# One ring of 17 half-size places for the second product's reads, eight steps ahead, and TensorE's order there as written

## The chip, the cores and the metric

One core of a Trainium2 chip runs the whole kernel. The time is the device time of one execution in microseconds (us), taken as the median of several; the kernel before has a median of 612.07 us over three runs (610.14 to 614.16). The engines are named as the profile names them: PE is TensorE's matrix multiply, PEld its weight load, DVE VectorE, ACT ScalarE, POOL GpSimd, SP the queue that issues nearly all DMAs here.

## The reference

Retention attention (a linear attention with a decay per head), and after it a feed-forward layer whose activation is `h * relu6(h + 3) / 6`:

```
state = gamma * state + outer(k_t, v_t);  y_t = scale * q_t @ state      # 4 batches, 8 heads, 768 tokens, 64 wide
x = y laid out as (3072 tokens, 512)
h = x @ w_in                      # (3072, 2048)
g = h * clip(h + 3, 0, 6) / 6
out = g @ w_out                   # (3072, 512)
```

All in float32.

## The kernel before

**Number format.** TensorE multiplies in the chip's reduced fp32r format. `split` (L130) turns a float32 tile into a high part (ACT, L131) and a low part, the rest (DVE, L132), and every product of two tiles is three matmuls: high by high, high by low, low by high. One matmul here is 128x128 weights by 512 columns.

**First product (up to L369).** Tokens are taken in six units of 512. Attention makes x for a unit, in pieces, between the matmuls of the unit before. `mm1` (L328) makes one 128x512 tile of h in 12 matmuls; ACT and DVE turn it into g (L337, L338), and SP stores it to DRAM (L339), into `gd[j]`, where j counts 8 pairs of 128 rows, at the place of the token unit and of the half (0 or 1) of the pair. PE's order is fixed to the order of the code there (`manual_schedule`, L343, closed at L368). The last unit's matmuls end at about 364 us.

**Second product (from L372).** It is done for three pairs of token units (u, v) by a scheme with seven instead of eight block products. A pair goes through four sweeps s, and a sweep through the eight j; one (pair, sweep, j) is a *step*:

- s = 0 reads g(u,0) and g(u,1), and makes products 1 and 2 from them
- s = 1 reads g(v,0), g(v,1), g(u,0); DVE makes s1 = g(v,0) + g(v,1), s2 = s1 - g(u,0), s3 = g(u,0) - g(v,0); products 6 and 7 from s2 and s3. s1 and s2 stay in `keep`
- s = 2 reads g(u,1); DVE subtracts s2; products 5 and 3 from s1 and that difference
- s = 3 reads g(v,1) for two j in one step; product 4

So a pair has 8 + 8 + 8 + 4 = 28 steps, and each step is two 128x512 operands, split into four tiles (one `gc` of 128x2x2x512), and 12 matmuls: 84 steps, 1008 matmuls. When a sweep ends, `evict` (L457) adds its PSUM banks into output tiles on ACT and DVE, and stores those that are complete.

The reads (`load_g`, L384) go into three kinds of tile: `gr` (two operands of 512 columns, 512 KB, two buffers in the pool `late`) for s = 0 and 3, `gr2` (three operands, two buffers) for s = 1, `gr3` (one, two buffers) for s = 2. `gc` has four buffers, two in each of the pools `late` and `rest`. `late` lies in memory that is free before the last token unit (L354); `rest` opens after the first product's pools are closed, and a tile of it waits for what lay at its place (`reuse_waits="tile"`).

The first two steps are read and split ahead of everything (L500, high priority); two more are read (L504), and then the loop at L507 prepares step n + 2 and reads step n + 4 with each step n (`SOON, FAR = 2, 4`, L486). DVE's instructions for them are placed behind `end`, the last DVE instruction of the first product (`issue_after`). The order of each engine's and queue's instructions, PE's in the second product too, is made by a scheduler from priorities, its own estimates of durations and the buffers that are free; every engine and SP then takes its instructions strictly in that order, and an instruction that waits holds up those behind it.

Of the kernel before, what the change touches and what calls it, by code (L numbers as in the profile page):

```python
# [9 lines left out]
F32 = mybir.dt.float32  # L10
# [9 lines left out]
P = 128  # L20
# [8 lines left out]
def retention_ffn(ctx: ExitStack, tc: tile.TileContext, qkv, w_in, w_out, dvs, dqs, out, B, H, S, D):  # L29
# [6 lines left out]
    nc = tc.nc  # L36
# [8 lines left out]
    UT = UR * P  # L45
# [16 lines left out]
    gd = [dram.tile([P, NU, 2, UT], F32, name=f"gd{j}") for j in range(NFP)]  # L62
# [8 lines left out]
        out=mask, in_=mask, pattern=[[1, P]], compare_op=ALU.is_ge, fill=0.0, base=0, channel_multiplier=-1  # L71
# [8 lines left out]
    def nm(s):  # L80
        return f"{s}_{next(serial)}"

    def dve_sub(out_, a, b):
        return nc.vector.tensor_tensor(out=out_, in0=a, in1=b, op=ALU.subtract)  # L84

    def dve_add(out_, a, b):
        nc.vector.tensor_tensor(out=out_, in0=a, in1=b, op=ALU.add)  # L87
# [42 lines left out]
    def split(hi, lo, src):  # L130
        nc.scalar.activation(out=hi, in_=src, func=AF.Copy)  # L131
        nc.vector.tensor_tensor(out=lo, in0=src, in1=hi, op=ALU.subtract)  # L132
# [187 lines left out]
    def advance(n):  # L320

        nonlocal done
        while done < min(n, NROW + 2):
            next(gen)
            done += 1
# [16 lines left out]
    order = ExitStack()  # L342
# [8 lines left out]
    for n, (u, jj) in enumerate(steps):  # L351
        if (u, jj) == (NU - 1, 0):
            att.close()
            late = ctx.enter_context(tc.tile_pool(name="late", bufs=1, side="right", reuse_waits="tile"))  # L354
# [10 lines left out]
            advance(2 * UR + 2 + int((jj + 1) / NF * UR + 0.5))  # L365
        elif 1 < u < NU - 1:
            advance(UR * (u + 1) + 2 + int((jj + 1) / NF * UR + 0.5))
    order.close()  # L368
    ph1.close()  # L369


# [4 lines left out]
    rest = ctx.enter_context(tc.tile_pool(name="rest", bufs=1, reuse_waits="tile"))  # L376
# [4 lines left out]
    work = [(b, s, j) for b in range(NB) for s in range(4) for j in range(0, NFP, 1 + (s == 3))]  # L381
    raws, gcs, banks, outs = {}, {}, {}, {}

    def load_g(step):  # L384

        b, s, j = step
        if s == 1:
            t = rest.tile([P, 3, UT], F32, tag="gr2", name=nm("gr2"), bufs=2)
            nc.sync.dma_start(out=t[:, 0], in_=gd[j][:, 2 * b, 0])
            nc.sync.dma_start(out=t[:, 1:3], in_=gd[j][:, 2 * b + 1])  # L390
        elif s == 2:
            t = rest.tile([P, UT], F32, tag="gr3", name=nm("gr3"), bufs=2)
            nc.sync.dma_start(out=t, in_=gd[j][:, 2 * b, 1])
        else:
            t = late.tile([P, 2, UT], F32, tag="gr", name=nm("gr"), bufs=2)
            if s == 0:
                nc.sync.dma_start(out=t, in_=gd[j][:, 2 * b])
            else:
                for i in range(2):
                    nc.sync.dma_start(out=t[:, i], in_=gd[j + i][:, 2 * b + 1, 1])  # L400
        raws[step] = t

    def sums(step):

        b, s, j = step
        t = raws.pop(step)
        s1, s2 = keep[j], keep[NFP + j]
        if s == 1:
            a11, a21, a22 = (t[:, i] for i in range(3))
            s3 = rest.tile([P, UT], F32, tag="s3", name=nm("s3"), bufs=2)  # L410
            dve_add(s1, a21, a22)
            dve_sub(s2, s1, a11)
            dve_sub(s3, a11, a21)
            raws[step] = (s2, s3)
        elif s == 2:
            dve_sub(t, t, s2)
            raws[step] = (s1, t)
        else:
            raws[step] = t

    def split_g(step, n):

        t = raws.pop(step)
        gc = (late, rest)[n // 2 % 2].tile([P, 2, 2, UT], F32R, tag="gc", name=nm("gc"), bufs=2)
        if isinstance(t, tuple):
            for i in range(2):
                split(gc[:, i, 0], gc[:, i, 1], t[i])
        else:
            split(gc[:, :, 0], gc[:, :, 1], t)
        gcs[step] = gc  # L430

    def mm2(step, hs):

        b, s, j = step
        gc = gcs[step]
        for h in hs:
            for q in range(2):
                i = SWEEPS[s][q if s < 3 else 0]
                jj = j if s < 3 else j + q
                if (b, i, h) not in banks:  # L440
                    banks[b, i, h] = ps_o[s % 2].tile([P, UT], F32, tag=f"o{2 * h + (q if s < 3 else 0)}", name=nm("o"))
                for n, (a, c) in enumerate(((0, 0), (0, 1), (1, 0))):
                    nc.tensor.matmul(  # L443
                        banks[b, i, h],
                        w2c[jj][:, RIGHT[i], a, h],
                        gc[:, q, c],
                        start=jj == 0 and n == 0,
                        stop=jj == NFP - 1 and n == 2,
                        skip_group_check=True,
                    )  # L450

    def store(b, mh, th, h, t, cols=slice(0, UT)):
        m = (2 * mh + h) * P
        t0 = (2 * b + th) * UT
        nc.sync.dma_start(out=out[m : m + P, t0 + cols.start : t0 + cols.stop], in_=t[:, cols])

    def evict(b, s, h, cols=(slice(0, UT),)):  # L457

        def add(out_, i, other, f=SIXTH, cut=slice(0, UT)):
            nc.vector.scalar_tensor_tensor(  # L460
                out=out_[:, cut], in0=banks[b, i, h][:, cut], scalar=f, in1=other[:, cut], op0=ALU.mult, op1=ALU.add
            )

        if s == 0:
            outs[h] = rest.tile([P, UT], F32, tag=f"u2_{h}", name=nm("u2"))
            nc.scalar.activation(out=outs[h], in_=banks[b, 1, h], func=AF.Copy, scale=SIXTH)
            c11 = rest.tile([P, UT], F32, tag="c11", name=nm("c11"), bufs=2)
            add(c11, 2, outs[h])
            store(b, 0, 0, h, c11)
        elif s == 1:  # L470
            outs[2 + h] = rest.tile([P, UT], F32, tag=f"u3_{h}", name=nm("u3"))
            add(outs[h], 6, outs[h])
            add(outs[2 + h], 7, outs[h])
        elif s == 2:
            c22 = rest.tile([P, UT], F32, tag="c22", name=nm("c22"), bufs=2)
            add(c22, 5, outs[2 + h])
            store(b, 1, 1, h, c22)
            add(outs[h], 5, outs[h])
            add(outs[h], 3, outs[h])
            store(b, 1, 0, h, outs[h])  # L480
        else:
            for cut in cols:
                add(outs[2 + h], 4, outs[2 + h], -SIXTH, cut)
                store(b, 0, 1, h, outs[2 + h], cut)

    SOON, FAR = 2, 4  # L486
    loaded, ready = iter(work), enumerate(work)

    def load_next():
        step = next(loaded, None)  # L490
        if step:
            load_g(step)

    def prepare_next():
        n, step = next(ready, (0, None))
        if step:
            sums(step)
            split_g(step, n)
# [8 lines left out]
    for n, step in enumerate(work):  # L507
        b, s, j = step
        last = b == NB - 1 and s == 3
        if last and j:  # L510
            break
        with tc.issue_after(end):
            for _ in range(NFP if last else 1):
                prepare_next()
                load_next()
        if not last:
            mm2(step, range(2))
            if work[n + 1][1] != s:
                for h in range(2):
                    evict(b, s, h)  # L520
            continue
        for h in range(2):
            for later in work[n:]:
                mm2(later, (h,))
            evict(b, s, h, (slice(0, UT),) if h == 0 else (slice(0, UT // 2), slice(UT // 2, UT)))


def constants(H, S, D):
# [56 lines left out]
```

## Time and profile before

| | |
|---|---|
| time, median of three | 612.07 us |
| the profiled execution's own time | 611.56 us |
| its span, first to last instruction | 609.8 us |
| PE busy / DVE / ACT / POOL | 589.7 / 433.5 / 249.6 / 20.6 us |
| first product's matmuls (L333) | 1152, to about 364 us |
| second product's matmuls (L443) | 1008, starts from 364.1 to 605.7 us |
| read and written in DRAM | 90.73 MB, 31.46 MB |

A row of the groups by line has the line, engine, operation, tiles out<-in, shapes and count, then the busy time and the mean of one in ns, then the idle time of the engine just before, and what ended it. The timeline has start and duration in us and merges neighbours of a kind; in brackets stands the idle time before the first of them. A row of the stretches has, for each engine, busy time and count, then PE's granted clock (1.00 is full), the mean busy share of the DMA engines, and GB/s. Matmuls overlap in the pipeline: a row of one matmul says 392 ns, but the next starts earlier than that.

### The profile page before, as it was taken

How to read it: one execution, taken by the hardware profiler on the slowest of the kernel's cores; microseconds unless marked ns; L12 is line 12 of the kernel's file. 1: busy time of each engine (PE TensorE's matmuls, PEld its weight loads, DVE VectorE, ACT ScalarE, POOL GpSimd, SP SyncE). 2: the span in 40 equal slices, each digit the busy share in tenths (PEclk: the TensorE clock that was granted, in tenths of full speed). 3: DMA queues.
4: the chain of work that ended last, by engine and by line, in shares of the span. 5: the costliest groups of instructions: out<-in, count | busy, mean ns of one | idle time of the engine just before them, and what ended most of it. 6: DMA issues, size and time to landing. Idle time of an engine off the chain costs nothing.

```text
span 609.8 us, 9211 instructions
## 1 busy us (share of the span) xinstructions
PE 589.7 (97%) x3436; PEld 485.7 (80%) x3436; DVE 433.5 (71%) x715; ACT 249.6 (41%) x426; POOL 20.6 (3%) x24
## 2 busy tenths in 40 slices
PE   7699999999999999999999999999999999999996
PEld 7677888888888888888888888868767888768884
DVE  4879999999333696333336966999857898548864
ACT  5765454544222442222225543444235433243440
POOL 0001000000000020000000000000000000000000
PEclk8989999999999999999999999999999999999999
DMA  8966778567544467454345428974857756757242
GB/s 320 390 226 206 241 236 265 191 207 254 195 156 162 167 207 243 170 166 162 125 136 175 157 103 283 308 234 126 307 174 212 235 175 204 234 174 250 53 119 104
DMA packets 55916, 122.79 MB, mean 201 GB/s; under 512 B 6336, under 2 KB 6592, under 8 KB 55872
## 3 DMA queue, kind: packets, MB, share of 16 engines
q1 hardware_dynamic: 55728, 122.18, 60.8%
q8 instruction: 27, 0.44, 0.3%
q14 instruction: 17, 0.14, 0.1%
q10 hardware_dynamic: 144, 0.02, 0.0%
HBM read 90.73 MB, written 31.46 MB: 200 GB/s over the span
## 4 chain that ended last, share of the span: by engine, by line
PE 49%; DVE 27%; DMA 16%; issue 3%; ACT 3%; SPq 1%; DVEq 0%; ACTq 0%
PE h L333 30%; DMA gr<-gd 13%; PE o L443 12%; DVE gc L132 6%; DVE g L338 2%; ACT gc L131 2%; PE y L247 2%; PE sc L243 2%; DVE we L122 2%; DMA st<-in_w_in 2%; DVE wb L119 2%; DVE am L284 2%; DVE w L132 2%; PE y L236 2%; DVE ww L125 2%
## 5 line engine op out<-in xcount | busy, mean ns | idle before, releaser
L333 PE MATMUL h<-x,w 128*128 128x512 f32 x1152 | 270.3, 394 | 3.4 <-ACT x L131 2.3
L333 PEld LDWEIGHTS h<-x,w 128*128 128x128 f32 x1152 | 215.6, 189 | 51.1 <-ACT x L131 2.7
L443 PE MATMUL o<-gc,w 128*128 128x512 f32 x1008 | 235.1, 393 | 6.8 <-DVE gc L132 6.5
L443 PEld LDWEIGHTS o<-gc,w 128*128 128x128 f32 x1008 | 187.9, 188 | 53.9 <-DVE gc L132 12.0
L338 DVE SCALAR_TENSOR_TENSOR g<-g,h 128x512 f32<-128x512 f32 x96 | 65.6, 684 | 85.0 <-ACT g L337 85.0
L337 ACT ACTIVATE g<-h,three 128x512 f32<-128x512 f32 x96 | 65.5, 685 | 107.3 <-PE h L333 103.8
L131 ACT ACTIVATE gc<-gr 128x1024 fp32r<-128x1024 f32 (+1 forms) x60 | 52.7, 886 | 91.0 <-DMA gr<-gd 60.7
L132 DVE TENSOR_TENSOR gc<-gr,gc 128x1024 fp32r<-128x1024 f32 (+1 forms) x60 | 60.0, 1008 | 36.4 <-ACT gc L131 36.0
L131 ACT ACTIVATE gc<-keep 128x512 fp32r<-128x512 f32 x48 | 29.7, 624 | 25.3 <-DVE keep L84 13.2
L131 ACT ACTIVATE w<-ww 128x384 fp32r<-128x384 f32 (+2 forms) x34 | 18.7, 555 | 43.8 <-DVE ww L125 41.3
L132 DVE TENSOR_TENSOR gc<-keep,gc 128x512 fp32r<-128x512 f32 x48 | 32.5, 685 | 1.0 <-ACT gc L131 1.0
L284 DVE TENSOR_TENSOR am<-sc,mask 128x1024 f32<-128x1024 f32 x24 | 29.2, 1216 | 0.0
L214 POOL TENSOR_TENSOR vn<-vn,cst_sb 128x512 f32<-128x512 f32 x16 | 19.9, 1241 | 271.5 <-DMA vn<-in_qkv 202.4
L117 ACT ACTIVATE we<-we,ebias 128x512 int32<-128x512 int32 x32 | 22.9, 717 | 14.2 <-DVE we L113 14.2
L460 DVE SCALAR_TENSOR_TENSOR u<-o,u 128x512 f32<-128x512 f32 (+1 forms) x31 | 20.1, 666 | 5.8 <-PE o L443 5.8
L125 DVE SCALAR_TENSOR_TENSOR ww<-wb,we 128x512 f32<-128x512 f32 x32 | 23.5, 734 | 0.7
L131 ACT ACTIVATE gc<-s 128x512 fp32r<-128x512 f32 x24 | 15.0, 625 | 20.9 <-DVE s L84 20.9
L87 DVE TENSOR_TENSOR keep<-gr 128x512 f32<-128x512 f32 x24 | 16.5, 688 | 9.3 <-DMA gr<-gd 9.2
L119 DVE SCALAR_TENSOR_TENSOR wb<-st,wb 128x512 f32<-128x512 uint32 x32 | 21.9, 686 | 0.2
L122 DVE SCALAR_TENSOR_TENSOR we<-st,we 128x512 int32<-128x512 int32 x32 | 21.9, 685 | 0.0
L132 DVE TENSOR_TENSOR w<-ww,w 128x384 fp32r<-128x384 f32 (+2 forms) x34 | 19.9, 592 | 2.7 <-ACT w L131 2.6
L280 ACT ACTIVATE state<-uz 128x512 f32<-128x512 f32 x20 | 11.8, 590 | 22.7 <-PE uz L271 22.7
(50 smaller groups left out, 389.1 us busy)
## 6 DMA issues: line engine op xcount, KB each, us to landing
gd<-g SPq DMA_DIRECT2D x96, 256.0 KB, 2.4
gr<-gd SPq DMA_DIRECT2D x48, 512.0 KB, 4.6
gr<-gd SPq DMA_DIRECT2D x72, 256.0 KB, 3.2
st<-in_w_in SPq DMA_DIRECT2D x16, 512.0 KB, 4.4
st<-in_w_out SPq DMA_DIRECT2D x16, 512.0 KB, 3.8
early<-in_qkv SPq DMA_DIRECT2D x28, 256.0 KB, 6.0
kn<-in_qkv SPq DMA_DIRECT2D x16, 256.0 KB, 4.4
kt<-in_qkv SPq DMA_DIRECT2D x16, 256.0 KB, 4.4
```

Of the source, the lines that this page charges most:

```text
L117: nc.scalar.activation(out=e, in_=e, func=AF.Relu, scale=8.0, bias=ebias)
L119: nc.vector.scalar_tensor_tensor(out=y, in0=lo.bitcast(U32), scalar=2.0**-32, in1=b, op0=ALU.mult, op1=ALU.add)
L122: nc.vector.scalar_tensor_tensor(out=e, in0=hi, scalar=-2147483648, in1=e, op0=ALU.bitwise_and, op1=ALU.bitwise_or)
L125: nc.vector.scalar_tensor_tensor(out=w, in0=y, scalar=2.0**-20, in1=e.bitcast(F32), op0=ALU.mult, op1=ALU.mult)
L131: nc.scalar.activation(out=hi, in_=src, func=AF.Copy)
L132: nc.vector.tensor_tensor(out=lo, in0=src, in1=hi, op=ALU.subtract)
L284: nc.vector.tensor_tensor(out=new["am"].rearrange("p h a n -> p (h a) n"), in0=sc.rearrange("p h a n -> p (h a) n"), in1=mask[:, None, :]. ...
L333: nc.tensor.matmul(h, t[:, o, a], xs[u][b][:, k], start=k + n == 0, stop=(k, n) == (NK - 1, 2), skip_group_check=True)
L337: nc.scalar.activation(out=g, in_=h, func=AF.Relu, bias=three)
L338: ins = nc.vector.scalar_tensor_tensor(out=g, in0=g, scalar=6.0, in1=h, op0=ALU.min, op1=ALU.mult)
L443: nc.tensor.matmul(banks[b, i, h], w2c[jj][:, RIGHT[i], a, h], gc[:, q, c], start=jj == 0 and n == 0, stop=jj == NFP - 1 and n == 2, skip_ ...
L460: nc.vector.scalar_tensor_tensor(out=out_[:, cut], in0=banks[b, i, h][:, cut], scalar=f, in1=other[:, cut], op0=ALU.mult, op1=ALU.add)
```

## The change

`load_g` reads every operand as its own DMA of 512 columns (256 KB) into its own tile. The tiles come from one sequence of 17 places: of 17 in a row the first four are `gl` tiles in `late` (four buffers), the other thirteen are `gr` tiles in `rest`. s3 of sweep 1 is written over g(u,0) in its place and no longer has a tile, the two output tiles c11 and c22 share two buffers, `split_g` splits every operand by itself (two instructions of 512 columns on ACT and on DVE for one of 1024), reads run up to eight steps ahead (`FAR = 8`), and `order.close()` moves to the end, so that PE takes the second product's matmuls in the order of the code too. The gc buffers (four) and the two steps of `SOON` stay.

```diff
-    order.close()
+
     ph1.close()
@@ load_g
-        if s == 1:
-            t = rest.tile([P, 3, UT], F32, tag="gr2", name=nm("gr2"), bufs=2)
-            nc.sync.dma_start(out=t[:, 0], in_=gd[j][:, 2 * b, 0])
-            nc.sync.dma_start(out=t[:, 1:3], in_=gd[j][:, 2 * b + 1])
...
+        if s == 0:
+            need = ((j, u, 0), (j, u, 1))
+        elif s == 1:
+            need = ((j, v, 0), (j, v, 1), (j, u, 0))
         elif s == 2:
+            need = ((j, u, 1),)
         else:
+            need = ((j, v, 1), (j + 1, v, 1))
+        raws[step] = []
+        for i, unit, half in need:
+            pool, tag, bufs = (late, "gl", 4) if next(slots) % 17 < 4 else (rest, "gr", 13)
+            t = pool.tile([P, UT], F32, tag=tag, name=nm("gr"), bufs=bufs)
+            nc.sync.dma_start(out=t, in_=gd[i][:, unit, half])
+            raws[step].append(t)
@@ sums, s == 1
-            s3 = rest.tile([P, UT], F32, tag="s3", name=nm("s3"), bufs=2)
             dve_add(s1, a21, a22)
             dve_sub(s2, s1, a11)
-            dve_sub(s3, a11, a21)
-            raws[step] = (s2, s3)
+            dve_sub(a11, a11, a21)
+            raws[step] = (s2, a11)
@@ split_g
-            split(gc[:, :, 0], gc[:, :, 1], t)
+        for i, t in enumerate(raws.pop(step)):
+            split(gc[:, i, 0], gc[:, i, 1], t)
@@
-    SOON, FAR = 2, 4
+    SOON, FAR = 2, 8
@@ end of the second product
+    order.close()
```

What now stands where, at two places. SP, the end of the first product: `gd` rows are its stores of g, `gr` the reads (the first number counts the tiles). The last of the stores and the reads behind it, before:

```order
L339 DMA gd7_70<-g_560_3445 128x512
L389 DMA gr2_580_3556<-gd0_63 128x512
L390 DMA gr2_580_3556<-gd0_63 128x1024
L397 DMA gr_568_3484<-gd4_67 128x1024
L397 DMA gr_574_3505<-gd5_68 128x1024
```

The same place now:

```order
L339 DMA gd7_70<-g_560_3445 128x512
L402 DMA gr_608_3658<-gd6_69 128x512
L402 DMA gr_567_3484<-gd2_65 128x512
L402 DMA gr_568_3486<-gd2_65 128x512
L402 DMA gr_569_3488<-gd3_66 128x512
L402 DMA gr_570_3490<-gd3_66 128x512
L402 DMA gr_571_3492<-gd4_67 128x512
```

Before, steps 2 and 3 of sweep 0 (from gd2 and gd3) had been read earlier, between the stores, and here stood sweep 1's first step and then j = 4 and 5. Now the reads of j = 2 and 3 stand behind the last store, and ahead of them one operand of sweep 1's j = 6 (gr_608). The four reads that stand earlier in their stead are of sweep 1:

```order
 L339 DMA gd7_70<-g_493_3028 128x512
-L397 DMA gr_565_3477<-gd2_65 128x1024
+L402 DMA gr_581_3515<-gd0_63 128x512
+L402 DMA gr_582_3517<-gd0_63 128x512
 L339 DMA gd7_70<-g_495_3045 128x512
-L397 DMA gr_566_3479<-gd3_66 128x1024
+L402 DMA gr_588_3540<-gd1_64 128x512
+L402 DMA gr_589_3542<-gd1_64 128x512
```

The two 512 KB reads of j = 2 and 3 are gone from here; four 256 KB reads for sweep 1's j = 0 and 1 took their place.

PE, the end of the first pair's sweep 0 (o is a PSUM bank, w2 the weights; gc_579 is j = 6, gc_581 j = 7, gc_584 sweep 1's first), before:

```order
L443 MATMUL o_572_3498<-gc_577_3536,w2_504_3122 128x512 x3
L443 MATMUL o_596_3659<-gc_584_3593,w2_199_1267 128x512 x3
L443 MATMUL o_569_3486<-gc_579_3553,w2_523_3231 128x512
L443 MATMUL o_570_3490<-gc_579_3553,w2_523_3231 128x512
L443 MATMUL o_571_3494<-gc_579_3553,w2_523_3231 128x512
L443 MATMUL o_572_3498<-gc_579_3553,w2_523_3231 128x512
L443 MATMUL o_597_3663<-gc_584_3593,w2_199_1267 128x512 x2
```

The same place now (gc_595 is j = 5, gc_599 j = 6):

```order
L438 MATMUL o_586_3531<-gc_595_3581,w2_504_3122 128x512 x3
L438 MATMUL o_583_3519<-gc_599_3604,w2_523_3231 128x512 x3
L438 MATMUL o_584_3523<-gc_599_3604,w2_523_3231 128x512 x3
L438 MATMUL o_585_3527<-gc_599_3604,w2_523_3231 128x512 x3
L438 MATMUL o_586_3531<-gc_599_3604,w2_523_3231 128x512 x3
```

Before, five matmuls of sweep 1 stood among those of sweep 0's seventh step; now every step's twelve stand together, three to a bank.

More of the change, by code (lines that the diff above doesn't have):

```diff
@@ L382, in retention_ffn @@
     raws, gcs, banks, outs = {}, {}, {}, {}
+    slots = iter(range(1 << 30))
     def load_g(step):
         b, s, j = step
-        if s == 1:
-            t = rest.tile([P, 3, UT], F32, tag="gr2", name=nm("gr2"), bufs=2)
-            nc.sync.dma_start(out=t[:, 0], in_=gd[j][:, 2 * b, 0])
-            nc.sync.dma_start(out=t[:, 1:3], in_=gd[j][:, 2 * b + 1])
+        u, v = 2 * b, 2 * b + 1
+        if s == 0:
+            need = ((j, u, 0), (j, u, 1))
+        elif s == 1:
+            need = ((j, v, 0), (j, v, 1), (j, u, 0))
@@ L391, in load_g @@
         elif s == 2:
-            t = rest.tile([P, UT], F32, tag="gr3", name=nm("gr3"), bufs=2)
-            nc.sync.dma_start(out=t, in_=gd[j][:, 2 * b, 1])
-        else:
[L395 to L401, printed above, removed]
+            need = ((j, u, 1),)
+        else:
+            need = ((j, v, 1), (j + 1, v, 1))
@@ L403, in sums @@
+        raws[step] = []
[4 more added lines that the diff above has]
+            raws[step].append(t)
     def sums(step):
         b, s, j = step
-        t = raws.pop(step)
+        t = raws[step]
         s1, s2 = keep[j], keep[NFP + j]
         if s == 1:
-            a11, a21, a22 = (t[:, i] for i in range(3))
-            s3 = rest.tile([P, UT], F32, tag="s3", name=nm("s3"), bufs=2)
+            a21, a22, a11 = t
@@ L411, in sums @@
             dve_add(s1, a21, a22)
             dve_sub(s2, s1, a11)
-            dve_sub(s3, a11, a21)
-            raws[step] = (s2, s3)
+            dve_sub(a11, a11, a21)
+            raws[step] = (s2, a11)
         elif s == 2:
[L416 to L419, printed above, removed]
+            dve_sub(t[0], t[0], s2)
+            raws[step] = (s1, t[0])
     def split_g(step, n):
-        t = raws.pop(step)
         gc = (late, rest)[n // 2 % 2].tile([P, 2, 2, UT], F32R, tag="gc", name=nm("gc"), bufs=2)
[L425 to L428, printed above, removed]
-            split(gc[:, :, 0], gc[:, :, 1], t)
+        for i, t in enumerate(raws.pop(step)):
+            split(gc[:, i, 0], gc[:, i, 1], t)
@@ L466, in evict @@
             nc.scalar.activation(out=outs[h], in_=banks[b, 1, h], func=AF.Copy, scale=SIXTH)
-            c11 = rest.tile([P, UT], F32, tag="c11", name=nm("c11"), bufs=2)
+            c11 = rest.tile([P, UT], F32, tag="c", name=nm("c11"), bufs=2)
             add(c11, 2, outs[h])
@@ L474, in evict @@
         elif s == 2:
-            c22 = rest.tile([P, UT], F32, tag="c22", name=nm("c22"), bufs=2)
+            c22 = rest.tile([P, UT], F32, tag="c", name=nm("c22"), bufs=2)
             add(c22, 5, outs[2 + h])
```

## The prediction

> **What bounds the kernel now.** I read the page first, then the second product's matmuls by line, their timeline, the stretches between their gaps, and the reads.
>
> ```profile
> PE 589.7 (97%) x3436; PEld 485.7 (80%) x3436; DVE 433.5 (71%) x715; ACT 249.6 (41%) x426; POOL 20.6 (3%) x24
> L443 PEld LDWEIGHTS o<-gc,w x1008: 186/188/193, 363.9 to 605.5; 128*128 128x128 f32 x168
> L443 PEld LDWEIGHTS o<-gc,w x245: 187/188/188, 465.9 to 521.8; 128*128 128x128 f32 x123
> ```
>
> PE is the bound: 97% busy. But a busy PE need not be at its pace. Weight loads, one for each matmul, tell the pace: in an undisturbed stretch 244 steps from one load to the next take 55.9 us, 0.2291 us each. All 1008 take 605.5 - 363.9 = 241.6 us for 1007 steps; at the pace that is 230.7. So the second product loses **10.9 us** to waits, and no change of reads or order can win more. Its timeline says where:
>
> ```profile
> 364.14 33.36 PE L443 MATMUL o<-gc,w 128*128 128x512 f32 x145
> 399.01 50.74 PE L443 MATMUL o<-gc,w 128*128 128x512 f32 x216 [1.51 <-DVE gc L132]
> 450.51 5.80 PE L443 MATMUL o<-gc,w 128*128 128x512 f32 x24 [0.76 <-DVE gc L132]
> 456.74 5.78 PE L443 MATMUL o<-gc,w 128*128 128x512 f32 x24 [0.43 <-DVE gc L132]
> 463.09 66.53 PE L443 MATMUL o<-gc,w 128*128 128x512 f32 x288 [0.56 <-DVE gc L132]
> 529.83 2.99 PE L443 MATMUL o<-gc,w 128*128 128x512 f32 x12 [0.22 <-DVE gc L132]
> 533.36 3.42 PE L443 MATMUL o<-gc,w 128*128 128x512 f32 x12 [0.54 <-DVE gc L132]
> 537.54 5.79 PE L443 MATMUL o<-gc,w 128*128 128x512 f32 x24 [0.75 <-DVE gc L132]
> 543.79 54.04 PE L443 MATMUL o<-gc,w 128*128 128x512 f32 x234 [0.47 <-DVE gc L132]
> 599.12 6.96 PE L443 MATMUL o<-gc,w 128*128 128x512 f32 x29 [1.29 <-DVE gc L132]
> ```
>
> A row loses the time to the next row's start less its matmuls at 0.2291. In order: 1.65 (399.01 - 364.14 - 145 x 0.2291), 2.01, 0.73, 0.85, 0.76, 0.78, 1.43, 0.75, 1.72, and 0.17 within the last 29: 10.85 together. Four places: the first pair (364 to 450: 3.7, some 0.9 of it in the wait before 450.51, which is the second pair's sweep 0 already), the rest of that sweep 0 (450 to 463: 1.6), sweep 0 of the third (463 to 544: 3.7), the last sweep (1.9).
>
> All these waits name DVE's split, but DVE isn't the cause in sweep 0. The stretches, the waits of ACT and SP, and the landing times show it:
>
> ```profile
> 398.00:444.00 46.00, 44.91 (x194) 35.96 (x195) 42.14 (x65) 19.29 (x28) 0.00 (x0) 1.00 0.65 211
> 444.00:464.00 20.00, 18.19 (x76) 13.77 (x75) 9.63 (x11) 7.09 (x8) 0.00 (x0) 1.00 0.62 184
> 524.00:544.00 20.00, 17.89 (x73) 12.98 (x72) 8.55 (x8) 6.36 (x6) 0.00 (x0) 1.00 0.64 185
> ACT gc L131 <- DMA gr<-gd: 59.5, 24, 6.3
> SPq L397 <- DVE gc L132: 36.5, 20, 2.4
> gr<-gd SPq DMA_DIRECT2D x48, 512.0 KB, 4.6
> gr<-gd SPq DMA_DIRECT2D x72, 256.0 KB, 3.2
> ```
>
> From 444 to 464 and 524 to 544 DVE is busy under half of the time (9.63 and 8.55 of 20 us), ACT waits for reads, and SP's reads (L397) wait for the split that frees one of only two buffers. A buffer's round is the read, 4.6 us, then ACT 1.06 and DVE 1.22 (the split rows below): 6.9 us for two steps' worth of buffers, 3.4 a step, where PE takes 12 x 0.2291 = 2.75. In 398 to 444, the first pair's sweep 1, it is otherwise: DVE is busy 42.14 of 46.
>
> **The change part by part.** *Reads up to eight steps ahead in 17 places.* Sweep 0 takes two places a step, so the ring holds eight steps, against two. A read then has some 8 x 2.75 = 22 us instead of about 5.5, and the longest of the landings quoted below is 6.6. Sweep 0 of pairs two and three and the last sweep are freed: 0.9 + 1.6 + 3.7 + 1.9 = 8.1 us. What is late next there is the split itself: gc has four buffers, as before, so a split follows PE's release by three steps, 8.2 us, and needs 2 x 0.63 + 0.69.
>
> *Two splits of 512 for one of 1024.*
>
> ```profile
> L132 DVE TENSOR_TENSOR gc<-gr,gc 128x1024 fp32r<-128x1024 f32 x34 | 41.4, 1223 | 33.9 <-ACT gc L131 33.8
> L131 ACT ACTIVATE gc<-gr 128x1024 fp32r<-128x1024 f32 x34 | 35.8, 1059 | 64.7 <-DMA gr<-gd 59.5 <-DVE keep L87 2.8 <-PE o L443 2.3
> L132 DVE TENSOR_TENSOR gc<-gr,gc 128x512 fp32r<-128x512 f32 x24 | 16.4, 686 | 1.0 <-ACT gc L131 0.7
> L131 ACT ACTIVATE gc<-gr 128x512 fp32r<-128x512 f32 x24 | 15.0, 627 | 25.1 <-DVE gr L84 25.1
> ```
>
> 36 of them (24 in sweep 0, 12 in sweep 3; two run before this window) cost DVE 2 x 0.686 - 1.223 = 0.15 us each, 5.4 in all, in the sweeps where it is least busy: nothing on the path; without that cover it would be a few tenths.
>
> *More DMAs.* 168 reads for 120. An issue keeps SP 0.4 us (0.38 and 0.45 below), so 19 us more spread over 240: hidden, since reads have steps in hand.
>
> *The start, which gets worse.* This is the one added wait. PE takes the first two steps, 24 matmuls, until 364.14 + 24 x 0.2291 = 369.6. Before, steps 2 and 3 had been read by then; now their places are in `rest`, and their reads stand behind the last store of g and behind gr_608. That one takes the place of gr_589, which DVE's first sum frees; the sum follows the last g.
>
> ```profile
> 365.06 0.69 DVE L338 SCALAR_TENSOR_TENSOR g<-g,h 128x512 f32<-128x512 f32 x1 [2.03 <-ACT g L337]
> 366.19 0.38 SPq L389 DMA_DIRECT2D gr<-gd  x1
> 366.62 0.45 SPq L390 DMA_DIRECT2D gr<-gd  x1
> 371.56 0.69 DVE L87 TENSOR_TENSOR keep<-gr 128x512 f32<-128x512 f32 x1 [3.19 <-DMA gr<-gd]
> 372.17 0.69 DVE L84 TENSOR_TENSOR s<-gr 128x512 f32<-128x512 f32 x1
> DMA to landing us min/median/max: 3.0/3.8/6.6
> 366.00:372.00 6.00, 6.00 (x28) 4.90 (x27) 2.80 (x3) 0.93 (x1) 0.00 (x0) 1.00 0.89 266
> 372.00:378.00 6.00, 6.00 (x28) 4.94 (x27) 4.83 (x7) 2.12 (x2) 0.00 (x0) 1.00 0.87 303
> ```
>
> The last g ends at 365.75, the sum at 366.4, and gr_608 is issued then; its landing takes 3.0 us (L389's shortest, the third row from below): 369.4. The reads behind it follow at the rate of this stage, 303 GB/s, 0.262 MB in 0.87 us: the first operand of step 2 lands at 370.3, the second at 371.2. With ACT 0.63 and DVE 0.69 PE can begin at about 371.7 and has the second operand at 372.6, three matmuls later. The stall is 2.1 to 2.4 us; I take **2.4**. Bounds: a read issued at 366.2 with 3.0 alone gives 366.2 + 3.0 + 1.3 - 369.6 = 0.9; the longest landing (6.6) for the read after gr_608 (366.85) gives 5.1. After step 2 each step needs two operands, 1.74 us, against PE's 2.75: no second stall.
>
> *Sweep 1 of the first pair, PE in written order.* A step there is three sums and two low parts on DVE. From one to the next is 0.61 us (372.17 - 371.56), so 3.05 us a step against 2.75: eight steps fall behind by 2.4 us, plus two evictions (1.2). Against that stands the lead. After the stall PE leaves sweep 0 at 364.14 + 96 x 0.2291 + 2.4 = 388.5, while the operands, one every 0.87 us from 370.3, are there for sweep 0 by 379.9 and for sweep 1's first two steps by 381.6; DVE has both steps split by 386 and the next two's sums begun. A lead of at least one step (2.75) plus the three steps in gc is more than 3.6. I take 0.7 us for this and for small waits elsewhere, between 0 and the 2.8 lost there now (3.7 less 0.9).
>
> *Sum*, on the profiled execution's own 611.56 (1.76 around the span of 609.8): 611.56 - 10.85 + 2.4 + 0.7 = 603.8. The median of three is 0.5 above that execution: **604.3**. The bounds give 611.56 - 10.85 + 0.9 + 0 = 601.6 and 611.56 - 10.85 + 5.1 + 2.8 = 608.6, with the 0.5 added 602.1 and 609.1.
>
> **The rivals.** *A: DVE sets the pace in the first sweep 1.* PE's old order took five matmuls of sweep 1 among sweep 0's seventh step; now PE stands still until its own next tile is there. If the lead is not there, the 2.4 + 1.2 fall due in place of 0.7: 607.2. For it: DVE busy 42.14 of 46. Against: that stretch had reads issued only from 366.19 on with two buffers. Chance 0.20.
>
> *B: slower.* Half-size reads with a lower rate. The second product moves 168 reads and 24 stores of 0.262 MB, 50.3 MB, in 241.6 us now: 208 GB/s. At over 1.26 us a piece DMA becomes the bound; at 1.35 it takes 259 us and the kernel 612 + 18 = 630. The row against: a 256 KB read lands in 3.2 us where 512 KB takes 4.6, so doubling costs 1.4 us and about 1.8 is fixed; pieces that queue behind each other hide that, as at 303 GB/s. For it speaks only that this stage mixes both sizes. The Trainium skill's page "DMA: Bandwidth & Descriptors" (Bandwidth) says to gather DMAs to 1 MiB or more for 75% of peak, which speaks against this change; by its fixed 2 us or so, 48 more DMAs one after another would be an estimated 96 us. The fixed 1.8 above agrees with its size, and the 303 GB/s show it overlapped. Chance 0.05.
>
> *C: the stall at the start lets PE's clock drop.*
>
> ```profile
> 0.00:50.00 50.00, 40.87 (x428) 35.63 (x430) 35.73 (x58) 32.90 (x93) 2.38 (x10) 0.93 0.87 311
> ```
>
> From a cold start the granted clock averages 0.93 over 50 us, up to 3.5 us lost; after the 1.51 us wait at 399 it stayed 1.00 (398 to 444). If a wait of 2.4 us drops it, that is 3.5 more: 607.8. It decides at some length over 1.51 that no row here shows. "TensorE: Matmul & The Clock Gate" of the Trainium skill (What's actually happening) puts that at an idle window of about 3.4 us, over my 2.4; so by it the clock stays. Chance 0.05.
>
> *D: the ring doesn't run ahead.* A place is free only when its operand is split, splits are held by four gc buffers, and SP's queue holds reads behind stores that wait for an eviction. If reads still come just in time, the 8.1 stay: 604.3 + 8.1 = 612.4, no difference. Against: sweeps 2 and 3 need one and two operands a step, so the ring fills there, and behind a sweep's stores a whole sweep passes before the reads after them are due. Chance 0.07.
>
> **How the numbers follow.** The forecast has 0.63, centred on 604.3, 602.1 to 607 in itself. All of B and D (0.12) and the forecast's upper end may be left out: 601.8 to 608.6 for 8 in 10, the lower end a little under the bound for the spread of the runs (610.14 to 614.16). One per cent is 6.1 us, and about what a measurement of this kernel can tell from no change; faster means below 605.9. Of the forecast 0.57 lies there, and 0.05 of A: 0.62. Within 1% are the rest of A and of the forecast, C and D and a little of B: 0.33. Slower is B: 0.05.
>
> **What would show it.** In the changed profile: PE's gaps between 444 and 464 and between 524 and 544 gone, so that from about 390 on the weight loads keep 0.229 us; the wait before the last 29 matmuls gone; one PE wait of 2 to 2.5 us at 369.6, behind ACT's split that waits for a read; SP's waits for L132 no longer followed by an ACT wait for DMA in the later pairs; DVE's 512-column splits at 0.69. Wrong would be PE waits in the first sweep 1 (A), reads landing later than 6 us at under 210 GB/s with PE waiting (B), a granted clock under 1.00 after 372 (C), or ACT waiting for reads in sweeps 0 (D). The prediction falls if the total lost by PE in the second product, 10.9 now, is over 6 or under 1.5.

## The result, and the profile after

The changed kernel takes 605.57 us (median of four; 603.93 at the least) where the kernel before, run beside it, takes 612.35. The ratio is 0.9882, with an interval of 0.9836 to 0.9928: faster by 1.2%. In a second comparison it was 603.85 us and 0.9854 (0.9811 to 0.9896), in a third 603.9 us and 0.9842 (0.9806 to 0.9877). In the first comparison the profiled execution had a granted clock of 0.752 from end to end (733.31 us; the median of the other three is 605.15, and the ratio goes by them), so the profile shown here is that of the second, whose own time is 605.32 us for a span of 603.6.

The page's first line, the row of the second product's weight loads in the view of one line (count, least, median and longest ns, first and last start), the matmuls' timeline over the whole second product, and the two waits of ACT that come first:

```profile
PE 589.0 (98%) x3436; PEld 488.3 (81%) x3436; DVE 435.0 (72%) x751; ACT 255.6 (42%) x462; POOL 17.9 (3%) x24
L438 PEld LDWEIGHTS o<-gc,w x1008: 185/188/330, 363.9 to 599.2; 128*128 128x128 f32 x168
364.17 5.68 PE L438 MATMUL o<-gc,w 128*128 128x512 f32 x24
371.06 0.50 PE L438 MATMUL o<-gc,w 128*128 128x512 f32 x1 [1.20 <-ACT gc L131]
371.78 1.31 PE L438 MATMUL o<-gc,w 128*128 128x512 f32 x3 [0.23 <-DVE gc L132]
373.32 226.51 PE L438 MATMUL o<-gc,w 128*128 128x512 f32 x980 [0.23 <-DVE gc L132]
ACT gc L131 <- PE o L438: 88.0, 58, 1.7
ACT gc L131 <- DMA gr<-gd: 6.2, 2, 5.3
```

Ten rows have become four. From 373.32 on 980 matmuls follow each other without a wait: the gaps from 399 to 464, from 530 to 544 and the one before the last 29 matmuls are gone. What is left is one place at the start. Of ACT's waits for reads, 59.5 us at 24 places, two are left, both there; ACT now waits for PE to free a `gc` tile (88.0 us), so the reads are ahead and the split is paced by PE. From 363.9 to 599.2 are 235.3 us; 1007 steps at 0.2291 are 230.7, so 4.6 us are lost where 10.9 were.

Two stretches in which PE had gaps before, now, and the one in which most reads of the first pair come in:

```profile
444.00:464.00 20.00, 20.00 (x89) 16.37 (x88) 19.48 (x33) 8.33 (x15) 0.00 (x0) 1.00 0.94 318
524.00:544.00 20.00, 20.00 (x89) 16.41 (x88) 18.71 (x31) 8.56 (x15) 0.00 (x0) 1.00 0.91 298
370.00:385.00 15.00, 13.44 (x48) 10.09 (x49) 11.14 (x18) 7.88 (x13) 0.00 (x0) 0.89 1.03 375
```

From 444 to 464 DMA moves 318 GB/s where it moved 184, and DVE is busy 19.48 of 20 us where it was 9.63: it now works ahead, on later steps, behind a PE that does not stop.

The start, by the timeline of all engines (some rows, in order of time):

```profile
365.10 0.69 DVE L338 SCALAR_TENSOR_TENSOR g<-g,h 128x512 f32<-128x512 f32 x1 [2.03 <-ACT g L337]
365.70 0.68 DVE L87 TENSOR_TENSOR keep<-gr,gr 128x512 f32<-128x512 f32 x1
366.41 7.15 SPq L402 DMA_DIRECT2D gr<-gd  x13
370.37 0.63 ACT L131 ACTIVATE gc<-gr 128x512 fp32r<-128x512 f32 x1 [5.31 <-DMA gr<-gd]
371.91 1.98 ACT L131 ACTIVATE gc<-gr 128x512 fp32r<-128x512 f32 x3 [0.91 <-DMA gr<-gd]
```

The last g, DVE's sum, gr_608 at 366.41 and the other reads behind it stand as forecast. The first operand of step 2 is there at 370.37, the second at 371.91. PE has done 28 matmuls by 373.32; without a wait it would have by 364.17 + 28 x 0.2291 = 370.58, and its weight loads, which start 0.2 us earlier, by 370.36. The wait is 3.0 us long by the loads.

A surprise lies right behind it, in PE's granted clock (the third column from the right). The bounds are those of a window of 3.41 us, and the next two:

```profile
370.18:373.59 3.41, 2.03 (x5) 0.94 (x6) 1.71 (x3) 2.23 (x4) 0.00 (x0) 1.00 0.98 332
373.59:377.01 3.42, 3.42 (x9) 2.65 (x9) 3.31 (x6) 2.79 (x6) 0.00 (x0) 0.50 1.03 393
377.01:380.42 3.41, 3.41 (x16) 2.74 (x16) 1.59 (x3) 1.69 (x4) 0.00 (x0) 1.00 1.05 388
```

For 3.4 us the clock is halved, though PE is at work again; that is half of 3.4 or 1.7 us lost on top of the 3.0, which together are the 4.6 within 0.1.

### The profile page after: what moved, and what is told of

The parts are those of the page before. It is cut to its first block, busy times and chain, and to the rows that moved or that the text cites. A ratio compares the mean times of both kernels' runs of the same rounds, so it can differ in the third digit from the quotient of the medians.

```text
span 731.6 us, 9451 instructions
## 1 busy us (share of the span) xinstructions
PE 721.2 (99%) x3436; PEld 525.4 (72%) x3436; DVE 442.9 (61%) x751; ACT 255.9 (35%) x462; POOL 18.1 (2%) x24
## 4 chain that ended last, share of the span: by engine, by line
PE 95%; DMA 2%; DVE 1%; SPq 1%; ACT 0%; issue 0%; DVEq 0%
PE h L333 45%; PE o L438 38%; PE sc L243 4%; PE y L247 4%; PE y L236 3%; PE uz L271 1%; DMA st<-in_w_in 1%; DMA early<-in_qkv 1%; DMA gr<-gd 0%; SPq L202 0%; DVE am L284 0%; DVE xr L262 0%; DVE w L132 0%; DVE gc L132 0%; ACT g L337 0%
## 5 line engine op out<-in xcount | busy, mean ns | idle before, releaser
L333 PE MATMUL h<-x,w 128*128 128x512 f32 x1152 | 332.8, 458 | 2.5 <-ACT x L131 1.7
L333 PEld LDWEIGHTS h<-x,w 128*128 128x128 f32 x1152 | 228.0, 199 | 98.2 <-ACT x L131 1.9
L438 PE MATMUL o<-gc,w 128*128 128x512 f32 x1008 | 286.4, 456 | 0.2 <-DVE gc L132 0.2
L438 PEld LDWEIGHTS o<-gc,w 128*128 128x128 f32 x1008 | 200.3, 199 | 86.1 <-DVE gc L132 0.5
L132 DVE TENSOR_TENSOR gc<-gr,gc 128x512 fp32r<-128x512 f32 x120 | 79.6, 686 | 39.4 <-ACT gc L131 39.2
L131 ACT ACTIVATE gc<-gr 128x512 fp32r<-128x512 f32 x120 | 71.4, 622 | 73.2 <-PE o L438 56.3
L214 POOL TENSOR_TENSOR vn<-vn,cst_sb 128x512 f32<-128x512 f32 x16 | 17.3, 1081 | 331.7 <-DMA vn<-in_qkv 314.4
L122 DVE SCALAR_TENSOR_TENSOR we<-st,we 128x512 int32<-128x512 int32 x32 | 23.6, 737 | 0.0
L262 DVE TENSOR_TENSOR xr<-y,dq 128x512 f32<-128x512 f32 x16 | 11.0, 690 | 19.7 <-PE y L247 19.5
L243 PE MATMUL sc<-qt,kt 64*128 64x128 f32 x256 | 22.4, 320 | 0.0
```

What stands on the lines that cost most here:

```text
L122: nc.vector.scalar_tensor_tensor(out=e, in0=hi, scalar=-2147483648, in1=e, op0=ALU.bitwise_and, op1=ALU.bitwise_or)
L243: nc.tensor.matmul(sc[:, h, p], new["kt"][pr, p], new["qt"][pr, p], start=True, stop=True, skip_group_check=True)
L333: nc.tensor.matmul(h, t[:, o, a], xs[u][b][:, k], start=k + n == 0, stop=(k, n) == (NK - 1, 2), skip_group_check=True)
L438: nc.tensor.matmul(banks[b, i, h], w2c[jj][:, RIGHT[i], a, h], gc[:, q, c], start=jj == 0 and n == 0, stop=jj == NFP - 1 and n == 2, skip_ ...
```

## The experiments

**The changed kernel again.** No edit; it serves as the kernel to compare with, and for the profile above.

> The changed kernel once more, unaltered, for a profile at the full granted clock. Theory (reads far enough ahead; the start pays): 603.5 to 606 us; PE loses about 3 us in the second product against its pace (10.9 before), of which 2 to 2.5 in one wait two steps after the second product begins, behind a split that waits for a read. Rival A (DVE sets the pace in the first pair's sweep 1): the lost time lies in several waits some 24 to 46 us after the second product begins, and the start shows less than 1 us.

Measured: 603.85 us, ratio 0.9854 (0.9811 to 0.9896). No wait is left in the second product but the one at the start. PE loses 4.6 us there, more than the 3 expected, 1.7 of it by the clock.

**PE's order alone.** The kernel before, with only the line that closes the fixed order moved:

```diff
@@ end of the first product
-    order.close()
@@ end of the second product
+    order.close()
```

> The kernel before with only PE's order in the second product as written; reads, tiles and lead as before. Theory (the reads' lead is the gain, the order is worth nothing): within 1.5 us of before, PE waits in the second and third pair's sweep 0 as before, 1.5 and 3.5 us or so. Rival (the written order carries part of the gain): 2 us or more below before. Second rival (the old order filled gaps): 1.5 to 3 us above before, in a longer wait at the first pair's sweep 1.

Measured: 612.62 us, ratio 0.9986 (0.9959 to 1.0014). Its weight loads, some rows of the timeline:

```profile
381.78 0.19 PEld L443 LDWEIGHTS o<-gc,w 128*128 128x128 f32 x1 [0.34 <-ACT gc L131]
383.04 21.82 PEld L443 LDWEIGHTS o<-gc,w 128*128 128x128 f32 x96 [1.07 <-DVE gc L132]
...
467.59 65.91 PEld L443 LDWEIGHTS o<-gc,w 128*128 128x128 f32 x288 [0.44 <-DVE gc L132]
...
600.69 6.54 PEld L443 LDWEIGHTS o<-gc,w 128*128 128x128 f32 x29 [1.71 <-DVE gc L132]
```

All the waits of the later sweeps 0 and of the last sweep stay, and a new one shows at 381.8, where PE's old order filled in matmuls of sweep 1. The order wins nothing.

**The ring alone.** The change without that line (PE's order in the second product left to the scheduler).

```diff
@@ end of the first product
+    order.close()
@@ end of the second product
-    order.close()
```

> The change without the written order: the scheduler orders PE's matmuls in the second product, the ring of 17 and the lead of eight stay. Theory: within 1 us of the changed kernel, with the wait at the start of 2 to 2.5 us. Rival (the order matters): 2 us or more from the changed kernel, either way.

Measured: 603.16 us, ratio 0.9837 (0.9805 to 0.9868), the same as the whole change. Its start, in weight loads:

```profile
363.36 5.47 PEld L438 LDWEIGHTS o<-gc,w 128*128 128x128 f32 x24
370.16 0.30 PEld L438 LDWEIGHTS o<-gc,w 128*128 128x128 f32 x2 [1.33 <-ACT gc L131]
...
371.92 224.03 PEld L438 LDWEIGHTS o<-gc,w 128*128 128x128 f32 x978 [0.27 <-DVE gc L132]
```

The wait stays, a little shorter (30 loads at the pace end at 370.23, so 1.7 us). The whole gain comes without the order: it is that of the half-size reads in 17 places, which the next two experiments take apart.

**Smaller reads alone.** The kernel before, each read of 512 KB made two of 256 KB into the same tile:

```diff
-                nc.sync.dma_start(out=t, in_=gd[j][:, 2 * b])
+                for i in range(2):
+                    nc.sync.dma_start(out=t[:, i], in_=gd[j][:, 2 * b, i])
```

(and in the same way for the pair of operands in sweep 1)

> The kernel before with every read of 512 KB as two DMAs of 256 KB into the same tiles; two buffers, lead and PE's order as before. Theory (the two buffers are the limit): a step's two halves land at about the time of the whole, so 0 to 2 us below before, PE waits in the later sweeps 0 stay, 3 us or more together. Rival (the size of the DMAs carries the gain: the changed kernel's reads moved 386 GB/s from 372 to 384 where before moved 303 to 307): 4 us or more below before, with 380 GB/s in that stretch and PE's later waits mostly gone.

Measured: 609.54 us, ratio 0.9932 (0.9898 to 0.9967). Its loads by line, two of its waits and one stretch:

```profile
L445 PEld LDWEIGHTS o<-gc,w x1008: 186/188/191, 367.0 to 606.2; 128*128 128x128 f32 x168
ACT gc L131 <- DMA gr<-gd: 52.6, 22, 5.9
524.00:544.00 20.00, 17.58 (x72) 12.80 (x71) 8.55 (x8) 6.49 (x7) 0.00 (x0) 1.00 0.67 208
```

The second product loses 239.2 - 230.7 = 8.5 us in place of 10.9, and sweep 0 of the third pair stays as idle as it was. The ratio is worth 4.2 us (2.0 to 6.2), the second product of this execution 2.4. So a part of the gain is to be had without any more places; I had costed the smaller reads only as 48 further issues, and they do something on their own. That a read of half the size lands sooner (3.6 us by its page, 4.6 for 512 KB before) would explain it; it was not tried apart. The rate is not the reason: between 370 and 385 these reads move 308 GB/s, where the kernel before moved 305 and the change 375.

**Four steps ahead in the same ring.**

```diff
-    SOON, FAR = 2, 8
+    SOON, FAR = 2, 4
```

> The change with reads up to four steps ahead, as before, in the ring of 17. Theory (two buffers were the limit, not the four steps: a round of read, ACT and DVE is 6.9 us and four steps are 11): within 1.5 us of the changed kernel, no PE wait in the later sweeps 0. Rival (the eight steps carry the gain): 3 us or more above it, with PE waits in sweep 0 of pairs two and three.

Measured: 603.66 us, ratio 0.9834 (0.9791 to 0.9876). In its second product too there is no wait but that at the start:

```profile
362.79 5.47 PEld L438 LDWEIGHTS o<-gc,w 128*128 128x128 f32 x24
369.81 0.19 PEld L438 LDWEIGHTS o<-gc,w 128*128 128x128 f32 x1 [1.55 <-ACT gc L131]
...
371.55 224.51 PEld L438 LDWEIGHTS o<-gc,w 128*128 128x128 f32 x980 [0.48 <-DVE gc L132]
```

The kernel before ran four steps ahead as well, by its code; it had no places for them. With the smaller reads alone leaving 8.5 us, the number of places is what decides, not whether the code asks four or eight steps ahead. In the change each operand also has a place of its own, which its own split frees; the share of that was not tried apart from the number.

**The start mended.** The ring turned by four, so that steps 2 and 3 (operands 4 to 7) take the `late` places again, right behind steps 0 and 1:

```diff
-            pool, tag, bufs = (late, "gl", 4) if next(slots) % 17 < 4 else (rest, "gr", 13)
+            n = next(slots)
+            pool, tag, bufs = (late, "gl", 4) if n < 4 or (n - 4) % 17 < 4 else (rest, "gr", 13)
```

> The change with the ring turned by four places: the first eight operands, not four, go to the places in late, so that the reads of steps 2 and 3 stand between the first product's last stores again. Theory: the wait at the start goes, 2 to 2.5 us less than the changed kernel: 602 to 603.5. Rival (the wait at the start covers one that comes later, in the first sweep 1, where DVE needs more per step than PE): within 0.7 us of the changed kernel, with PE waits 24 to 46 us after the second product begins.

Measured: 600.36 us (600.03 to 602.1), ratio 0.9793 (0.9762 to 0.9824): the fastest of all, 3.5 us below the change in the same comparison. Its timeline over the second product, SP's reads before it, and the stretch behind its start:

```profile
314.52 1.77 SPq L403 DMA_DIRECT2D gr<-gd  x4
319.51 1.21 SPq L403 DMA_DIRECT2D gr<-gd  x2
322.23 0.92 SPq L403 DMA_DIRECT2D gr<-gd  x2
363.28 231.03 PEld L439 LDWEIGHTS o<-gc,w 128*128 128x128 f32 x1008
388.50:398.00 9.50, 9.50 (x43) 7.80 (x42) 9.50 (x17) 3.80 (x6) 0.00 (x0) 1.00 1.02 373
```

All 1008 weight loads stand in one row of 231.03 us, the pace itself. The reads of eight operands, the first four steps' own, are issued by 323.2, and PE never waits. The 3.5 us are more than the 2 to 2.5 expected; in the profile shown first the start lost 4.6. Its last row has DVE busy for all of 9.5 us with PE at its pace: the first sweep 1 goes through, but how narrowly does not show in it.

**How narrow DVE is in the first sweep 1.** The mended kernel with one more addition for each step of that sweep, into a tile that is not read again:

```diff
+            if b == 0:
+                dve_add(a22, a21, a22)
```

> The kernel with the ring turned by four places, which has no PE wait in the second product, and in the first pair's sweep 1 one more DVE addition in each of the eight steps (0.61 us from one to the next, 4.9 in all; its result, over an operand that is not read again, is not used). It measures how far DVE is ahead there. Theory (a lead of a step and three in gc: 2.4 + 1.2 fall behind now, at least that much is in hand): the sweep falls behind by 8.5 and PE waits for 1 to 4 us of the 4.9, in the second half of that sweep: 601.5 to 604.5. Rival A (DVE sets the pace there already, by a hair): all 4.9 on the path, 605 or more. Third possibility: a lead over 8.5, no PE wait.

Measured: 603.46 us, ratio 0.9831 (0.978 to 0.9883). That is above the mended kernel by 3.1 us in the medians and 2.3 in the ratios (they ran in different comparisons). The waits, in weight loads, first and last rows:

```profile
363.51 33.88 PEld L441 LDWEIGHTS o<-gc,w 128*128 128x128 f32 x148
398.02 1.91 PEld L441 LDWEIGHTS o<-gc,w 128*128 128x128 f32 x9 [0.63 <-DVE gc L132]
...
408.87 188.75 PEld L441 LDWEIGHTS o<-gc,w 128*128 128x128 f32 x824 [0.67 <-DVE gc L132]
```

Between 363.51 and 408.87 lie 184 loads, 42.15 us at the pace, so 3.2 us are lost. Eight additions of 0.61 are 4.9 us. So in the mended kernel DVE had about 1.7 us in hand at the end of that sweep: Rival A's mechanism is real, and was missed there by that much. The trace of the change itself shows nearly the same: at the tightest place of that sweep DVE's split is done at 406.02, and the weight load that needs it starts at 407.82, 1.8 us later; in the mended kernel the tightest has 1.5.

**The clock behind the wait, filled.** The change with ten matmuls between steps 1 and 2, into a bank that is overwritten afterwards; they only keep PE busy:

```diff
+            if n == 1:
+                idle = ps_o[1].tile([P, UT], F32, tag="o0", name="idle2")
+                for _ in range(10):
+                    nc.tensor.matmul(idle, w2c[1][:, 0, 0, 0], gcs[step][:, 0, 0],
+                                     start=True, stop=True, skip_group_check=True)
```

> The changed kernel with ten matmuls whose result is not used (gc and w2 tiles into a PSUM bank that sweep 1 has not opened yet) between step 1 and step 2 of the second product, 10 x 0.23 = 2.3 us, where PE waits for the reads. They stand for the wait; the reads come no earlier. Theory (the wait at the start also drops PE's granted clock in some executions, 0.86 and 0.80 from 370 to 380 in the profile of the changed kernel, 1.7 us): the clock stays 1.00 behind it, and the time is that of the changed kernel's better executions, 601.5 to 603.5, with less spread than its 601.4 to 607.7. Rival (the spread is of the chip and has nothing to do with the wait): same median and same spread as the changed kernel beside it, or 0.5 us more.

Measured: 604.4 us (603.28 to 605.51), ratio 0.9853 (0.9815 to 0.9892). Its profile has the wait filled and no drop of the clock behind it:

```profile
369.33 2.25 PEld L516 LDWEIGHTS idle<-gc,w 128*128 128x128 f32 x10
...
373.18 224.48 PEld L438 LDWEIGHTS o<-gc,w 128*128 128x128 f32 x980 [0.54 <-DVE gc L132]
```

The median did not fall as expected; it is 0.5 us above the change beside it, as the rival had it. Three executions lie from 603.28 to 603.54, three from 605.26 to 605.51, and the latter have the same granted clocks (0.994 and 0.997) as the former. So the clock is not the only cause of the spread; the other was not found. Part of it lies ahead of this change: in the profiles of the change and of its variants the second product's first weight load starts anywhere from 362.74 to 364.31.

**The changed kernel a third time**, in that comparison.

> The changed kernel unaltered, beside the kernel with its wait filled: 601 to 608 us in two groups, near 602 where the granted clock is 0.997 and near 606 where it is 0.99, if the drop behind the start's wait makes the spread; spread evenly about 604 if not.

Measured: 603.9 us, ratio 0.9842 (0.9806 to 0.9877). Here the profile has nearly the same waits and no drop. Two windows of 3.41 us around the wait, bounds again those of the clock's windows:

```profile
364.31 5.47 PEld L438 LDWEIGHTS o<-gc,w 128*128 128x128 f32 x24
371.24 0.19 PEld L438 LDWEIGHTS o<-gc,w 128*128 128x128 f32 x1 [1.46 <-ACT gc L131]
371.97 0.53 PEld L438 LDWEIGHTS o<-gc,w 128*128 128x128 f32 x3 [0.54 <-DVE gc L132]
372.82 224.47 PEld L438 LDWEIGHTS o<-gc,w 128*128 128x128 f32 x980 [0.32 <-DVE gc L132]
368.24:371.65 3.41, 2.38 (x10) 1.48 (x8) 0.43 (x1) 0.87 (x2) 0.00 (x0) 1.00 0.99 315
371.65:375.06 3.41, 3.18 (x14) 2.35 (x14) 2.17 (x4) 2.12 (x4) 0.00 (x0) 1.00 0.99 362
```

By 372.82 PE has had 28 loads, 370.73 at the pace, so this wait is 2.1 us. The windows cut it in two: ten matmuls run in the first, eight of which start in it, and fourteen in the second. In the profile shown first, a window held nearly all of the wait and five matmuls, and the clock dropped in the next. The six executions of this comparison lie from 602.12 to 605.10 without a gap between two groups. The fifteen executions of the changed kernel other than that of 733.31 us, with their mean granted clock, in order of the clock:

```
1.000: 603.93
0.997: 601.40 602.12 602.39
0.994: 603.46 604.34
0.993: 602.31 603.18
0.992: 605.99
0.991: 604.94
0.990: 605.10 605.15 605.32 606.90
0.988: 607.72
```

The eight at 0.993 and over have a median of 602.8, the seven below of 605.3. The mean clock doesn't say where in the kernel a half-clocked window lay, though: in both profiles of the change the first 40 us hold two already (the granted clock there is 0.91). The 2.5 us between the groups are more than the 1.7 that one window can cost, and of fifty executions of the kernel before, whose profile shows no drop in the second product, six are under 0.993 too. None of the six of the mended kernel, which doesn't wait at the start, is under 0.994; but neither is any of the ten with the ring alone or with four steps ahead, which waited 1.7 and 2.3 us in their profiles, under 0.993. So that the change pays a drop as well as the wait is shown for one execution; that it does so in about half of them is likely and not shown.

**A longer wait.** The change with the first operand of step 2 read twice, so that the wait grows by what one more read and its landing take:

```diff
-            nc.sync.dma_start(out=t, in_=gd[i][:, unit, half])
+            for _ in range(2 if step == work[2] and not raws[step] else 1):
+                nc.sync.dma_start(out=t, in_=gd[i][:, unit, half])
```

> The changed kernel with the first operand of step 2 read twice, the second read into the same tile after the first has landed, so that PE's wait at the start grows by 3 to 4 us to over 5. Theory (a wait of some 3 us or more drops the granted clock): a clock of 0.85 or less in the 8 us behind the wait, and 5 to 6 us above the changed kernel, 3.5 for the wait and 1.5 to 2 for the clock. Rival (drops come by chance, whatever the wait): 3 to 4 us above it, clock 1.00 behind the wait.

Measured: 608.9 us (606.24 to 611.17), ratio 0.9924 (0.9892 to 0.9955), above the change by 5.0 us in the medians and 4.3 in the ratios, both against the change's second comparison (they didn't run in the same one). The wait, and the clock's windows from it on:

```profile
373.32 0.29 PEld L439 LDWEIGHTS o<-gc,w 128*128 128x128 f32 x1 [5.11 <-ACT gc L131]
374.05 227.43 PEld L439 LDWEIGHTS o<-gc,w 128*128 128x128 f32 x983 [0.44 <-DVE gc L132]
368.65:372.06 3.41, 0.00 (x0) 0.00 (x0) 0.69 (x1) 0.63 (x1) 0.00 (x0) 1.00 0.98 333
372.06:375.47 3.41, 2.15 (x4) 1.45 (x5) 2.17 (x4) 2.75 (x6) 0.00 (x0) 0.50 0.96 320
375.47:378.88 3.41, 3.41 (x9) 2.64 (x8) 2.13 (x4) 1.18 (x2) 0.00 (x0) 0.50 1.09 378
378.88:382.29 3.41, 3.41 (x16) 2.78 (x15) 2.49 (x4) 1.58 (x3) 0.00 (x0) 1.00 0.98 357
```

By 374.05 PE has had 25 loads, 368.47 at the pace: a wait of 5.6 us, 2.6 longer than in the change. One window is empty, the next, in which PE works for the last 2.1 us, is half clocked, and so is the one behind that, in which PE is busy throughout; then the clock is full. From 374.05 to 378.88 PE works at half clock, 4.8 us, which loses 2.4 more: 8.0 us for this start, against 4.6 and, without a drop, 2.1 above.

**Smaller pieces still.** Each 256 KB read as two of 128 KB, so 336 reads:

```diff
-            nc.sync.dma_start(out=t, in_=gd[i][:, unit, half])
+            for c in range(2):
+                cols = slice(c * UT // 2, (c + 1) * UT // 2)
+                nc.sync.dma_start(out=t[:, cols], in_=gd[i][:, unit, half, cols])
```

> The change with every read as two DMAs of 256 columns (128 KB), 336 for 168. Theory (fixed costs of DMAs are hidden, since the reads are steps ahead and SP has time): within 1 us of the changed kernel, the wait at the start up to 0.5 us longer or shorter. Rival B (smaller DMAs cost rate): 5 us or more above it, SP busy with issues for 130 us or more and ACT waiting for reads in sweeps 0 and 1.

Measured: 605.16 us, ratio 0.9874 (0.9826 to 0.9921), 1.3 us above the change in the same comparison, which four executions don't tell from no difference (its interval overlaps that of the change, 0.9806 to 0.9877). SP's reads, the stretch from 370 to 385, and two waits:

```profile
365.90 30.23 SPq L404 DMA_DIRECT2D gr<-gd  x62
370.00:385.00 15.00, 13.75 (x50) 10.50 (x51) 10.52 (x16) 8.29 (x14) 0.00 (x0) 0.89 0.83 260
402.21 5.37 PEld L440 LDWEIGHTS o<-gc,w 128*128 128x128 f32 x24 [0.42 <-DVE gc L132]
408.23 191.47 PEld L440 LDWEIGHTS o<-gc,w 128*128 128x128 f32 x836 [0.65 <-DVE gc L132]
```

62 reads in 30.23 us are one every 0.488 us, with hardly a pause between them: 0.131 MB in that time is 269 GB/s, and 260 came of it, with DMA busy 0.83. So by these rows it is SP's issuing that bounds the rate here. Two waits in the first sweep 1 are new, 0.7 us together against the pace; reads that come later leave DVE less of a lead there, which would be their cause, but that wasn't shown apart. With 256 KB, DMA is busy throughout (1.03) at 375 GB/s. So Rival B's lower rate is there one size further down; that it costs more than the noise isn't shown.

## Why the prediction was right

604.3 was forecast, and 604.3 is the median of the fifteen executions, which lie from 601.40 to 607.72. By its steps:

- *PE's pace bounds, 10.9 us at the most to win.* Shown: the mended kernel has 1008 loads in 231.03 us and takes 600.36, where 611.56 - 10.85 = 600.7.
- *Reads ahead free 8.1 us in the later sweeps 0 and the last sweep.* Shown: those gaps are gone, and with PE's order alone they stay. Only the reason given for it, eight steps ahead, says too much: four do as well, in 17 places. And 2.4 of it (by one profile; 4.2 by the ratio) the kernel before wins by smaller reads alone.
- *2 x 512 splits, 48 more DMAs: nothing.* Shown; DVE's busy time rises by 1.5 us (433.5 to 435.0) where the sum had 5.4, and no wait of PE's answers to either. With twice as many DMAs again SP issues with hardly a pause.
- *The start wait, 2.4.* The mechanism was right to the instruction: the sum at 365.70, gr_608 at 366.41 (366.4 forecast), the first operand at 370.37 (370.3). The size was 3.0 in the profile shown, 2.1 in that of the third comparison, and 2.35 with four steps ahead (371.55 less the 28 loads from 362.79). The step that is off is the second operand 0.87 us behind the first, at the mean rate: ACT took it up 1.54 us behind in the first of these (370.37 and 371.91), and 0.85 behind in the second. PE did not stand still for all of it: it began at 371.06, on the high part alone, and it was the second operand that ended the wait.
- *0.7 for the first sweep 1.* It was nothing. DVE held the pace with 1.8 us in hand (about 1.7 in the mended kernel, by the added work); Rival A (0.20) did not come true, but with 4.9 us more on DVE there, in the mended kernel, it does, and costs 3.2.
- *Rival C, the clock, 0.05.* It came true in the execution shown, at 1.7 us a window, where I had put it at 3.5; how often else is open. The Trainium skill, "TensorE: Matmul & The Clock Gate" (What's actually happening), has a free-running window of 3413 ns and a drop after an idle one; the 3.41 us stretches above agree in length and in that they do not start with the wait. I had read the rule as one on the length of a wait, and from it "the clock stays". The profiles fit one on what a window contains: a wait of 3.0 us in three pieces, with five matmuls started within the window, was enough in the execution shown, and a window with eight was not. The longest single piece does not decide it, for that is 1.20 us of idle PE here, and behind the 1.51 at 399 in the kernel before the clock stayed. The sum of the pieces might: the waits of 3.0 us and more had the drop, those of 1.7 to 2.3 had not. The rule as the Trainium skill has it, one idle window, is met only in the longer wait.
- *D, the ring doesn't run ahead, and B.* Neither: ACT's waits for reads fell from 59.5 to 6.2 us, and DMA moved 375 GB/s, more than the 303 taken from before.

So the sum was right in its large terms, and in the small ones by luck as much as by working: 3.1 us were allowed for the start and the first sweep 1, and the start alone cost 2.1 without the clock's drop and 4.6 with it.

## What to carry to other kernels

When a buffer's round (read, split, free) is longer than the step it feeds, more places cure it, and how far ahead the code asks hardly matters; count the places, not the steps. Look where a new ring puts its *first* reads: which place each takes, and what must be done before that place is free; here turning the ring by four places was worth 3.5 us on top of the change's 9. And a wait of PE can cost a clock window of 1.7 us as well, as one of 3.0 us did here and those of 1.7 to 2.3 did not in the profiles, so taking the last wait away can win more than its length.

## What the runs showed of the hardware that was not expected

- The granted clock falls to one half for whole windows of 3.41 us (6.83 for two), by a grid that does not start with the wait: in the profile shown first one such window starts at 32.26 and one at 373.59, which is 341.33 us or 100 windows later. Behind a window with 5 matmuls of 512 columns it fell, and with 6 (the 128 KB pieces, 369.77 to 373.18); with 10 it stayed, twice (the third comparison, and the ring alone, 368.98 to 372.39), and with 8, twice (four steps ahead, and the kernel before at its wait at 399; seven of the eight start in the window):

```profile
367.33:370.74 3.41, 2.06 (x8) 1.15 (x8) 0.69 (x1) 1.23 (x2) 0.00 (x0) 1.00 0.94 321
397.27:400.68 3.41, 1.90 (x8) 1.41 (x8) 2.86 (x5) 1.03 (x2) 0.00 (x0) 1.00 0.60 221
```

  PE's busy time does not tell them apart (2.03 us in the first that fell, 1.90 in the last that stayed); the count does in these six, which is too few for a rule. A window without any, followed by one of 2.1 us of work, gave two half-clocked windows.
- 256 KB reads issued one after another moved 375 GB/s between 370 and 385, where the kernel before, with its mix of 256 and 512 KB in few places, moved 305, and 256 KB reads in those few places 308; 128 KB reads moved 260, with SP issuing one each 0.488 us with hardly a pause.
